# Loading the next input in four-row parts behind its scatters, in two standing buffers, with the weight stores one job later

## The chip, the cores and the metric

The kernel runs on one core of one Trainium2 chip. The metric is the device time of one execution in microseconds (us); a run's figure is the median over several executions. A core has TensorE (PE in the profile; its weight loads are PEld), VectorE (DVE), ScalarE (ACT), GpSimd (POOL) and SyncE (SP). SP issues most DMAs here and works its instructions off in order, so a DMA whose wait is not yet met holds all that stand behind it. POOL does the same with its own DMAs, the scatters and gathers.

## The reference

```python
X = np.fft.rfft(x, axis=1)                      # x: 8 inputs of 3072 rows x 256
Yr = Xr @ w_r - Xi @ w_i + b_r
Yi = Xr @ w_i + Xi @ w_r + b_i                  # then a soft threshold of 0.01 on both
y = np.fft.irfft(Y, n=3072, axis=1)             # 8 * 3072 = 24576 tokens
...
logits = xn @ en.T / tau                        # tokens routed to one of 8 experts
out[mask] = gate_w[mask, None] * (np.maximum(x[mask] @ w1[e], 0.0) @ w2[e])
...
h = x @ w_in                                    # dense layer over all tokens
return np.maximum(0.01 * h, h) @ w_out
```

## The kernel before

The program has three stages: the transform with the routing (up to about 910 us of the profile), the experts (to about 2173 us) and the dense layer (to the end). The change touches only the first, which takes the eight inputs b = 0 to 7 in turn.

An input has a **forward part**, `main_step(b, g)` for g = 0 to 25, and an **inverse part**, a loop over n2 = 0 to 36. `mix` (PE, L490) multiplies group g by the weights, ACT and DVE split the result into two halves (`split_evict`, L178 and L179), `s2` (L512) transforms it, DVE makes the threshold result `z` (L515 to L517), `s2i` (L528) starts back. In the inverse part PE transposes (`pv`, L540), finishes a row block n2 (`pyo`, L576), and DVE copies it into row n2 of the buffer `xt` of input b + 1 (L610), whose old content PE has read by then. The first transform of input b + 1 (`s1`, PE, L468) reads that buffer ahead of it: two row blocks each in the steps g = 24 and 25 and then one in each turn of the inverse loop, so that turn n2 reads row block n2 + 4. The first three steps of input b + 1 stand in the turns 31 to 33, so the forward loop proper begins with g = 3.

So a buffer `xt` goes through three uses: input b + 1 is loaded and read, the finished rows of input b are put in its place, and 32 indirect DMAs (`scatter`, POOL, L656) send them to their slots in DRAM while input b + 1 is worked on. From g = 3 to 24 a step issues one of them, two where g is a multiple of 3; the last two go out in the turns 5 and 6 of the inverse loop. A one-element copy on POOL (L655) holds each scatter until the `z` of the step before is there, which sets its pace. Input b + 2 can be loaded only where the rows have been scattered. In this version the pool `big` has two buffers of 16 row blocks; `load_x` takes a new one at q = 0 and 4, and such a buffer comes free as a whole. `refill` asks for the parts q = 0 to 3 (384 KB, four row blocks each) in the steps g = 21 to 24 and for 4 to 7 in the turns n2 = 4 to 7. Input 1 is loaded through the forward part of input 0, where no scatter goes out yet.

Beside it `split_job` prepares the experts' weights in 128 jobs, one a step up to g = 22 from input 0 on until none is left (in input 6). A job does three things in this order: SP loads a piece `wf` (128 KB, L451); then, for the piece of two jobs before, ACT makes the upper half of `hl` (L456), POOL the lower (L457); SP stores that `hl` (256 KB, L458). There are three buffers `wf` and four `hl`. On SP the store waits for POOL's half, on POOL that half stands behind the scatters of the step, and on ACT the upper half stands between the evictions that PE's results need.

Of the kernel before, what the change touches and what calls it, by code (L numbers as in the profile page):

```python
# [11 lines left out]
F32 = mybir.dt.float32  # L12
# [10 lines left out]
B, S, D = 8, 3072, 256  # L23
E = 8
T = B * S
N1, N2 = 96, 32
# [117 lines left out]
def build(ctx: ExitStack, tc: tile.TileContext, a: dict, out: bass.AP):  # L144
    nc = tc.nc
# [182 lines left out]
    def spectral(big, expert_start):  # L328
        with ExitStack() as st, ExitStack() as mst:
# [31 lines left out]

            xt = {}

            def load_x(b, q):
                if q % 4 == 0:
                    t = big.tile([128, 16, D], F32, tag="s", name="xt")
                    for j in range(4):
                        xt[b, q + j] = t[:N1, 4 * j:4 * j + 4, :]
                nc.sync.dma_start(
                    xt[b, q], x[b].rearrange("(p r) c -> p r c", r=N2)[:, 4 * q:4 * q + 4, :])  # L370

# [61 lines left out]
            jobs = []  # L433
            for e in range(E):
                for k in range(2):
                    for h in range(4):
                        o = k * 1024 + h * 256
# [4 lines left out]
                                 w2d[128 * e:128 * e + 128], f * 256))  # L442
            jobs.reverse()

            wait = []

            def split_job():
                if jobs:
                    src, dst, o = jobs.pop()
                    wf = m3.tile([128, 256], F32, tag="wf", name="wf")  # L450
                    nc.sync.dma_start(wf, src)  # L451
                    wait.append((wf, dst, o))
                if len(wait) == 3 or not jobs and wait:
                    wf, dst, o = wait.pop(0)
                    hl = m2.tile([128, 2, 256], F32R, tag="hl", name="hl", bufs=4)
                    nc.scalar.activation(hl[:, 0], wf, AF.Copy)  # L456
                    nc.gpsimd.tensor_tensor(hl[:, 1], wf, hl[:, 0], op=ALU.subtract)  # L457
                    nc.sync.dma_start(dst.rearrange("p (s n) -> p s n", s=2)[:, :, o:o + 256], hl.bitcast(F32))  # L458

            ps1 = {}  # L460

# [60 lines left out]
            def s2i(g):  # L522
                y = Y.pop(g)
                if g % 2 == 0:
                    pz[0] = psc.tile([128, 2, 2, 128], F32, tag="c", name="pz")
                p = pz[0]
                for db in range(2):
                    nc.tensor.matmul(p[:, db, g % 2, :], y[:, 128 * db:128 * db + 128], gi[:, g, :],  # L528
                                     start=True, stop=True)
                if g % 2 == 1:  # L530
                    nc.scalar.activation(
                        Z[:, :, :, 4 * g - 4:4 * g + 4],
                        p.rearrange("p b g (j n) -> p b n (g j)", n=N2), AF.Copy)
# [288 lines left out]


            LEAD = 2
            todo = []
            scat = []

            def main_step(b, g):
                last = b == B - 1
                if g == 3:  # L830

                    s2i(0)
                if g < NG:
                    mix(g)
                if 1 <= g <= NG:
                    s2(g - 1)
                if g >= NG and not last:
                    for _ in range(2):
                        s1(b + 1, lead[0])
                        lead[0] += 1  # L840
                if g >= 3:
                    s2i(g - 2)
                if b == 0 and g == 3:
                    todo.extend(prologue3())
                if g >= 3:
                    for _ in range(2):
                        if todo:
                            todo.pop(0)()
                if 2 <= g <= NG:
                    for _ in range(1 if g % 3 else 2):  # L850
                        scatter(Y[g - 1][0:1, 0:1])
                if 4 - (b > 0) <= g < 23:
                    split_job()
                if b == 0 and g % 3 == 1 and g // 3 < 8:
                    load_x(1, g // 3)
                if b and g in (21, 22, 23, 24):
                    refill(b + 1, g - 21)

            def scatter(step):
                if scat:  # L860
                    scat.pop(0)(step)
# [3 lines left out]
            def refill(b, q):  # L865


                if b < B:
                    load_x(b, q)
                elif q % 4 == 0:  # L870
                    w = q // 4
                    la[w][0] = big.tile([128, 4096], F32R, tag="s", name=f"W{w + 1}_0")
                    load_weights(0, w, la[w][0])
# [19 lines left out]
            for b in range(B):  # L893
# [4 lines left out]
                g0 = 0  # L898
                while lead[0] < LEAD and not last:
                    s1(b + 1, lead[0])  # L900
                    lead[0] += 1
                if last:
                    assert not jobs and not wait and not todo
                    mst.close()
                    yp = st.enter_context(tc.tile_pool(name="fy", bufs=1, reuse_waits="tile"))
                    y7.append(yp.tile([128, N2, D], F32, name="y7"))
                    ex = expert_start(la)
                    next(ex)
# [10 lines left out]
                for n2 in range(N2 + LAG + 2):  # L919
                    ready = len(squares)  # L920
                    copies()
                    if lead[0] < N2 and not last:
                        s1(b + 1, lead[0], later)
                        lead[0] += 1
                    if n2 < N2:
                        swap(n2, later)
                    if LAG <= n2 < N2 + LAG:
                        pend.append(s1i(b, n2 - LAG))
                    if ready:
                        squares.pop(0)()  # L930
                        if n2 < 10:
                            scatter(cur["ss"][0:1, n2 - LAG - 2:n2 - LAG - 1])
                    if n2 in (3, 9):
                        logits1(n2 // 9)
                    if n2 in (6, 12):
                        logits2(n2 // 12)
                    if n2 == 16:
                        logits = logits3()
                    if n2 == 17:
                        logits()  # L940
                        slots, sc, gates = routing(b)
                    if n2 > 17 and slots:
                        slots.pop(0)()
                    if n2 == 30:
                        assert not scat
                    if b and n2 in (4, 5, 6, 7):
                        refill(b + 1, n2)
                    if not last and n2 in MERGE:
                        copies()
                        main_step(b + 1, g0)  # L950
                        g0 += 1
                    if last and n2 >= 5 and n2 % 2 == 1:
                        copies()
                        next(ex)
# [195 lines left out]
    with tc.manual_schedule():  # L1150
        with ExitStack() as est:
# [7 lines left out]
            big = est.enter_context(tc.tile_pool(name="big", bufs=2, side="right"))  # L1159
# [38 lines left out]
```

## Time and profile before

| | |
|---|---|
| median of 3 runs | 4367.9 us (4366.33 to 4370.6) |
| the profiled execution, its own time | 4368.49 us |
| its span, first to last instruction | 4366.7 us |
| granted TensorE clock, mean over the span | 0.987 |
| PE busy / PEld / DVE / ACT / POOL | 98% / 87% / 55% / 43% / 14% |

The page cuts the span into 40 slices of 109 us each. PE is busy in nine tenths or more of nearly every slice, and the two lower digits are among the first eight slices, the stage that the change touches. The mean clock of 0.987 is not spread over the run either. A shared figure such as "98% busy" therefore says little about this stage: it is read in stretches of its own, one for each forward and each inverse part, by PE's busy time, the granted clock beside it, and the waits that ended PE's idle time. PE busy at half the clock counts as busy, so a stretch's length and its clock are read together.

### The profile page before, as it was taken

The page shows a single profiled execution, that of the slowest core. Times are in us where ns is not written, and L with a number is a line of the kernel's source. Part 1 is how long each engine was busy: PE and PEld are TensorE (multiplying, and loading weights), DVE is VectorE, ACT ScalarE, POOL GpSimd, SP SyncE. Part 2 cuts the span into 40 slices and gives each one's busy share as a digit, 9 for nine tenths or more (in the row PEclk, how much of TensorE's full clock was granted, in tenths as well). Part 3 has the DMA queues.
Part 4 walks back from the last instruction along what each step waited for, and adds up shares of the span by engine and source line. Part 5 has one row for each costly group of instructions (what it writes and reads, how often), then busy time and mean ns, then how long its engine had stood idle before and what let it go on. Part 6 is the DMA issues. An engine that isn't in the chain of part 4 may idle for free.

```text
span 4366.7 us, 72634 instructions
## 1 busy us (share of the span) xinstructions
PE 4271.0 (98%) x27214; PEld 3819.4 (87%) x27214; DVE 2391.4 (55%) x4977; ACT 1895.8 (43%) x4268; POOL 601.2 (14%) x893
## 2 busy tenths in 40 slices
PE   9989898999999999999999999999999999999999
PEld 8878787889999999999978888888888888888888
DVE  5777777763455555533355555555555555555554
ACT  4555555553333333333244444444444444444443
POOL 2443333424000000000010010100101000010100
PEclk9999999999999999999999999999999999999999
DMA  6343333242332225234100000000000000000000
GB/s 209 115 123 104 113 110 114 84 162 85 115 117 99 94 96 194 108 124 160 47 28 25 20 25 25 25 25 20 27 22 25 25 21 29 20 25 25 22 18 15
DMA packets 139074, 309.71 MB, mean 71 GB/s; under 512 B 21049, under 2 KB 72866, under 8 KB 134370
## 3 DMA queue, kind: packets, MB, share of 16 engines
q1 hardware_dynamic: 113250, 244.34, 16.6%
q0 software_dynamic: 25472, 60.73, 4.7%
q8 instruction: 215, 3.52, 0.4%
q14 instruction: 137, 1.12, 0.1%
HBM read 542.30 MB, written 115.02 MB: 151 GB/s over the span
## 4 chain that ended last, share of the span: by engine, by line
PE 88%; DVE 5%; DMA 2%; issue 2%; ACT 1%; POOL 1%; SPq 0%; another core or an unknown queue 0%; DVEq 0%; POOLq 0%; ACTq 0%
PE mpH L1035 24%; PE mpO L1060 16%; PE pO L272 14%; PE pH L256 14%; PE mpO L1061 8%; PE pu L490 3%; PE ps L468 2%; PE py L512 1%; PE pz L528 1%; DMA xt<-in_x_dram 1%; PE pyo L576 1%; DVE t L516 1%; DVE z L517 1%; DVE vl L543 1%; PE pT L240 1%
## 5 line engine op out<-in xcount | busy, mean ns | idle before, releaser
L1041 DVE TENSOR_TENSOR mg<-mpH,ms 128x512 f32<-128x512 f32 x768 | 531.4, 692 | 1046.5 <-ACT ms L1040 1041.1
L1060 PE MATMUL mpO<-W,mgh 128*128 128x512 f32 x3008 | 1095.9, 398 | 0.0
L1035 PE MATMUL mpH<-mxh,W 128*128 128x512 f32 x3072 | 1083.9, 394 | 4.8 <-DVE mg L1041 4.6
L1040 ACT ACTIVATE ms<-mpH 128x512 f32<-128x512 f32 x768 | 459.9, 599 | 1190.3 <-PE mpH L1035 977.6
L1061 PE MATMUL mpO<-W,mgl 128*128 128x256 f32 x3008 | 842.1, 280 | 0.0
L256 PE MATMUL pH<-xh,W 128*128 128x256 f32 x3296 | 728.9, 283 | 1.7 <-DMA W<-w1d 1.0
L1035 PEld LDWEIGHTS mpH<-mxh,W 128*128 128x128 f32 x3072 | 578.7, 188 | 144.2 <-DVE mg L1041 5.8
L1060 PEld LDWEIGHTS mpO<-W,mgh 128*128 128x128 f32 x3008 | 564.7, 188 | 132.4
L260 DVE SCALAR_TENSOR_TENSOR ehl<-pH,ehh 128x256 fp32r<-128x256 f32 x824 | 349.7, 425 | 600.7 <-ACT ehh L259 596.4
L259 ACT ACTIVATE ehh<-pH 128x256 fp32r<-128x256 f32 x824 | 316.3, 384 | 760.9 <-PE pH L256 743.6
L272 PE MATMUL pO<-W,ehh 128*128 128x256 f32 x3264 | 630.3, 285 | 0.4 <-issue 0.4
L1035 PE MATMUL mpH<-mxl,W 128*128 128x512 f32 x1536 | 606.7, 395 | 0.0
L1061 PEld LDWEIGHTS mpO<-W,mgl 128*128 128x128 f32 x3008 | 567.3, 189 | 24.9
L1008 POOL DMA_INDIRECT mxr<-ys,row x192 | 187.4, 976 | 2869.3 <-PE mpT L1020 1746.5
L256 PEld LDWEIGHTS pH<-xh,W 128*128 128x128 f32 x3296 | 573.7, 192 | 2.4 <-DMA W<-w1d 1.2
L1050 DVE TENSOR_TENSOR mgl<-mg,mgh 128x512 fp32r<-128x512 f32 x768 | 523.5, 682 | 0.0
L272 PEld LDWEIGHTS pO<-W,ehh 128*128 128x128 f32 x3264 | 508.2, 192 | 1.7 <-issue 1.7
L1049 ACT ACTIVATE mgh<-mg 128x512 fp32r<-128x512 f32 x768 | 479.0, 624 | 0.1
L256 PE MATMUL pH<-xl,W 128*128 128x256 f32 x1648 | 466.8, 283 | 0.0
L272 PE MATMUL pO<-W,ehl 128*128 128x256 f32 x1632 | 462.1, 283 | 0.9 <-issue 0.9
L1035 PEld LDWEIGHTS mpH<-mxl,W 128*128 128x128 f32 x1536 | 289.7, 189 | 33.1 <-DVE mxl L179 0.4
L256 PEld LDWEIGHTS pH<-xl,W 128*128 128x128 f32 x1648 | 316.5, 192 | 0.2 <-issue 0.2
(214 smaller groups left out, 5412.2 us busy)
## 6 DMA issues: line engine op xcount, KB each, us to landing
W<-w1d SPq DMA_DIRECT2D x101, 2048.0 KB
W<-w2d SPq DMA_DIRECT2D x101, 2048.0 KB
xg<-xs SPq DMA_DIRECT2D x103, 256.0 KB
ys<-eo SPq DMA_DIRECT2D x102, 256.0 KB
xt<-in_x_dram SPq DMA_DIRECT2D x64, 384.0 KB
out_dram<-mo SPq DMA_DIRECT2D x47, 512.0 KB
wf<-in_moe_w_dram SPq DMA_DIRECT2D x128, 128.0 KB
w1d<-hl SPq DMA_DIRECT2D x64, 256.0 KB
```

The costliest lines, as they stand in the source:

```text
L256: nc.tensor.matmul(p, l, r, start=(i == 0), stop=(i == 5))
L259: nc.scalar.activation(hh, p, AF.Relu)
L260: nc.vector.scalar_tensor_tensor(hl, p, 0.0, hh, op0=ALU.max, op1=ALU.subtract)
L272: nc.tensor.matmul(O[b][:, t, :], l, r, start=(f == 0 and i == 0 and t == 0), stop=(f == 7 and i == 2 and t == 1))
L1008: nc.gpsimd.indirect_dma_start(out=xr[i][:, t].bitcast(F32), out_offset=None, in_=ys, in_offset=IndirectOffsetOnAxis(ap=slot[:, 4 * i + t: ...
L1035: nc.tensor.matmul(p, l, r, start=(j == 0), stop=(j == 5))
L1040: nc.scalar.activation(s, p, AF.Copy, scale=0.01)
L1041: nc.vector.tensor_tensor(g, p, s, op=ALU.max)
L1049: nc.scalar.activation(gh, g, AF.Copy)
L1050: nc.vector.tensor_tensor(gl, g, gh, op=ALU.subtract)
L1060: nc.tensor.matmul(p, gh[:, c], wout[:, :, f], start=(f == 0), stop=False)
L1061: nc.tensor.matmul(p[:, 0], gl[:, c], wout[:, 0, f], start=False, stop=(f == 15))
```

## The change

The two buffers `xt` are now taken once and live through the stage, so that each part of four rows depends only on its own last users. The parts q = 0 to 6 of the next input but one are loaded in the steps g = 8, 11, 14, 17, 20, 22 and 25, two or three steps behind the scatter of their last row, and part 7 in turn 7 of the inverse loop. In the last input the first two expert weight buffers, which take the place of `xt`, are asked for at g = 17 and n2 = 7 instead of g = 21 and n2 = 4. A job's store is put into a list `done` and issued in the next job, behind that job's load of `wf`.

```diff
+            xbuf = [big.tile([128, 16, D], F32, tag="s", name="xt") for _ in range(2)]
+
             def load_x(b, q):
-                if q % 4 == 0:
-                    t = big.tile([128, 16, D], F32, tag="s", name="xt")
-                    for j in range(4):
-                        xt[b, q + j] = t[:N1, 4 * j:4 * j + 4, :]
+                xt[b, q] = xbuf[q // 4][:N1, 4 * (q % 4):4 * (q % 4) + 4, :]
                 nc.sync.dma_start(
                     xt[b, q], x[b].rearrange("(p r) c -> p r c", r=N2)[:, 4 * q:4 * q + 4, :])
...
-            wait = []
+            wait, done = [], []
...
                     wait.append((wf, dst, o))
+                if done:
+                    dst, o, hl = done.pop(0)
+                    nc.sync.dma_start(dst.rearrange("p (s n) -> p s n", s=2)[:, :, o:o + 256], hl.bitcast(F32))
                 if len(wait) == 3 or not jobs and wait:
                     wf, dst, o = wait.pop(0)
                     hl = m2.tile([128, 2, 256], F32R, tag="hl", name="hl", bufs=4)
                     nc.scalar.activation(hl[:, 0], wf, AF.Copy)
                     nc.gpsimd.tensor_tensor(hl[:, 1], wf, hl[:, 0], op=ALU.subtract)
-                    nc.sync.dma_start(dst.rearrange("p (s n) -> p s n", s=2)[:, :, o:o + 256], hl.bitcast(F32))
+                    done.append((dst, o, hl))
...
+            REFILL = (8, 11, 14, 17, 20, 22, 25)
...
-                if b and g in (21, 22, 23, 24):
-                    refill(b + 1, g - 21)
+                if b and g in REFILL:
+                    refill(b + 1, REFILL.index(g))
...
-                elif q % 4 == 0:
+                elif q % 4 == 3:
                     w = q // 4
...
-                    if b and n2 in (4, 5, 6, 7):
-                        refill(b + 1, n2)
+                    if b and n2 == 7:
+                        refill(b + 1, 7)
```

On SP, from g = 20 of input 1 to its inverse part, before (`xt` are the loads of input 2, `w1d<-hl` the stores; DMASW are the eight semaphores that the scatters use in turn, DMAHW those of SP's own DMAs):

```order
L451 DMA wf_2366<-in_moe_w1_dram 128x256 [waits DMAHW1_49]
L458 DMA w1d_57<-hl_2368 256x1x256 [waits DMAHW0_49,Pool_49]
L451 DMA wf_2402<-in_moe_w1_dram 128x256 [waits DMAHW3_49]
L458 DMA w1d_57<-hl_2404 256x1x256 [waits DMAHW2_49,Pool_49]
L369 DMA xt_2408<-in_x_dram 96x1024 [waits DMASW4_49,DMASW3_49,DMASW5_49,DMASW2_49,DMASW6_49,DMASW1_49,DMASW7_49,DMASW0_49,PE_49]
L451 DMA wf_2438<-in_moe_w1_dram 128x256 [waits DMAHW5_49,DMAHW4_49]
L458 DMA w1d_57<-hl_2440 256x1x256 [waits Pool_49]
L369 DMA xt_2408<-in_x_dram 96x1024 [waits DMAHW6_49]
L369 DMA xt_2408<-in_x_dram 96x1024 [waits DMAHW7_49]
L369 DMA xt_2408<-in_x_dram 96x1024 [waits DMAHW0_49]
L369 DMA xt_2582<-in_x_dram 96x1024 [waits DMASW4_49,DMASW5_49,DMASW3_49,DMASW6_49,DMASW2_49,DMASW7_49,DMASW1_49,DMAHW1_49,DMASW0_49,PE_49]
```

The same place after the change:

```order
L450 DMA wf_2367<-in_moe_w1_dram 128x256 [waits DMAHW3_49,DMAHW2_49,Pool_49]
L454 DMA w1d_57<-hl_2336 256x1x256
L368 DMA xt_136<-in_x_dram 96x1024 [waits DMASW2_49,DMASW3_49,DMASW1_49,DMAHW4_49,DMASW0_49,PE_49]
L450 DMA wf_2404<-in_moe_w1_dram 128x256 [waits DMAHW6_49,DMAHW5_49,Pool_49]
L454 DMA w1d_57<-hl_2370 256x1x256
L450 DMA wf_2438<-in_moe_w1_dram 128x256 [waits DMAHW7_49,DMAHW0_49,Pool_49]
L454 DMA w1d_57<-hl_2407 256x1x256
L368 DMA xt_136<-in_x_dram 96x1024 [waits DMASW6_49,DMASW7_49,DMASW5_49,DMAHW1_49,DMASW4_49,PE_49]
L368 DMA xt_136<-in_x_dram 96x1024 [waits DMASW2_49,DMASW3_49,DMASW1_49,DMAHW2_49,DMASW0_49,PE_49]
L368 DMA xt_136<-in_x_dram 96x1024 [waits DMASW6_49,DMASW7_49,DMASW5_49,DMAHW3_49,DMASW4_49,PE_49]
L665 DMA slotd_61<-mx_2841 96x32 [waits DMAHW4_49,DVE_49]
```

Here only the last four parts of input 2 are left, each waits for four scatters in place of eight, and the wait for POOL has gone from the store to the next load of `wf`.

On SP again, in the steps g = 6 to 9 of input 2, before:

```order
L451 DMA wf_3313<-in_moe_w2_dram 128x256 [waits DMAHW6_49,DMAHW5_49]
L458 DMA w2d_58<-hl_3315 256x1x256 [waits Pool_49]
L451 DMA wf_3347<-in_moe_w2_dram 128x256 [waits DMAHW7_49,DMAHW0_49]
L458 DMA w2d_58<-hl_3349 256x1x256 [waits Pool_49]
L451 DMA wf_3381<-in_moe_w2_dram 128x256 [waits DMAHW2_49,DMAHW1_49]
L458 DMA w2d_58<-hl_3383 256x1x256 [waits Pool_49]
L451 DMA wf_3417<-in_moe_w2_dram 128x256 [waits DMAHW5_49,DMAHW3_49]
```

After the change the same steps hold the first part of input 3:

```order
L450 DMA wf_3342<-in_moe_w2_dram 128x256 [waits DMAHW7_49,DMAHW6_49,Pool_49]
L454 DMA w2d_58<-hl_3311 256x1x256
L450 DMA wf_3376<-in_moe_w2_dram 128x256 [waits DMAHW1_49,DMAHW0_49,Pool_49]
L454 DMA w2d_58<-hl_3345 256x1x256
L368 DMA xt_135<-in_x_dram 96x1024 [waits DMASW2_49,DMASW3_49,DMASW1_49,DMAHW2_49,DMASW0_49,PE_49]
L450 DMA wf_3413<-in_moe_w2_dram 128x256 [waits DMAHW4_49,DMAHW3_49,Pool_49]
L454 DMA w2d_58<-hl_3379 256x1x256
```

A load of `xt` that waits for scatters now stands between two loads of `wf`; the stores stand behind the loads without a wait for POOL.

## Rows read from the trace of the kernel before

**Rows 1.** Waits of PE, inputs 1 to 6: waiter and releaser, total us, times, longest.

```profile
engine line waited for: us in total, times, longest us
PE ps L468 <- DMA xt<-in_x_dram: 30.9, 10, 5.4
PE pz L528 <- DVE z L517: 20.3, 41, 1.2
```

**Rows 2.** Windows: the inverse parts of the inputs 0 to 6, TensorE.

```profile
core 0: us, PE busy (x), PEclk, DMA share, GB/s
88.90:132.80 43.90, 41.57 (x358) 1.00 0.10 32
194.80:253.60 58.80, 49.89 (x358) 0.83 0.31 88
317.00:375.10 58.10, 50.33 (x357) 0.82 0.30 88
439.40:491.90 52.50, 44.52 (x358) 0.93 0.34 96
559.40:617.20 57.80, 50.55 (x357) 0.82 0.32 89
681.30:736.00 54.70, 45.73 (x357) 0.91 0.32 93
797.80:842.80 45.00, 41.80 (x358) 1.00 0.20 54
```

**Rows 3.** Windows: the forward parts of the inputs 1 to 6, same columns.

```profile
132.80:194.80 62.00, 59.65 (x365) 1.00 0.48 148
253.60:317.00 63.40, 59.96 (x366) 1.00 0.47 146
375.10:439.40 64.30, 59.95 (x366) 1.00 0.46 144
491.90:559.40 67.50, 62.42 (x364) 0.97 0.43 136
617.20:681.30 64.10, 59.97 (x365) 1.00 0.46 144
736.00:797.80 61.80, 59.44 (x367) 1.00 0.44 131
```

**Rows 4.** Timeline, input 1: SP's and PE's rows at the first load of input 2.

```profile
198.12 0.54 SPq L458 DMA_DIRECT2D w1d<-hl  x1
198.97 0.34 SPq L369 DMA_DIRECT2D xt<-in_x_dram  x1
...
203.64 0.74 PE L468 MATMUL ps<-f,xt 96*128 96x96 f32 x2 [4.94 <-DMA xt<-in_x_dram]
```

**Rows 5.** Windows of input 1 from that wait on, same columns.

```profile
198.70:203.60 4.90, 0.01 (x1) 0.67 0.87 243
203.60:217.40 13.80, 13.76 (x67) 0.50 0.35 104
```

**Rows 6.** Timeline: POOL's scatters of input 1 whose landing SP waits for.

```profile
150.46 0.92 POOL L656 DMA_INDIRECT xs<-xt,si  x1 [0.16 <-issue]
...
157.85 0.74 POOL L457 TENSOR_TENSOR hl<-wf,hl 128x256 fp32r<-128x256 f32 x1
...
222.44 0.92 POOL L656 DMA_INDIRECT xs<-xt,si  x1 [0.15 <-issue]
```

**Rows 7.** Timeline: the second four loads (SP), their first use, PE's rank product.

```profile
225.73 1.72 SPq L369 DMA_DIRECT2D xt<-in_x_dram  x4
...
229.61 0.66 PE L468 MATMUL ps<-f,xt 96*128 96x96 f32 x4 [1.91 <-DMA xt<-in_x_dram]
...
245.20 0.31 PE L650 MATMUL prk<-ob,tri 96*96 96x256 bf16 x1 [0.72 <-DVE ob L674]
```

**Rows 8.** Waits of ACT in the forward part of input 1.

```profile
ACT hl L456 <- DMA wf<-in_moe_w_dram: 9.9, 10, 2.2
```

**Rows 9.** Timeline, input 0: a load of input 1 ahead of a weight piece.

```profile
84.04 1.80 SPq L369 DMA_DIRECT2D xt<-in_x_dram  x1
85.95 0.36 SPq L451 DMA_DIRECT2D wf<-in_moe_w_dram  x1
...
89.81 0.42 ACT L456 ACTIVATE hl<-wf 128x256 fp32r<-128x256 f32 x1 [1.19 <-DMA wf<-in_moe_w_dram]
```

**Rows 10.** Timeline, input 1: a weight piece without such a load ahead.

```profile
182.10 0.60 SPq L451 DMA_DIRECT2D wf<-in_moe_w_dram  x1
...
185.25 0.42 ACT L456 ACTIVATE hl<-wf 128x256 fp32r<-128x256 f32 x1 [2.16 <-DMA wf<-in_moe_w_dram]
```

**Rows 11.** Timeline, input 4: a late scatter on POOL, then ACT, then PE.

```profile
517.76 0.93 POOL L656 DMA_INDIRECT xs<-xt,si  x1 [2.28 <-DVE t L516]
...
523.38 0.42 ACT L456 ACTIVATE hl<-wf 128x256 fp32r<-128x256 f32 x1 [3.35 <-DMA wf<-in_moe_w_dram]
...
527.14 0.71 PE L528 MATMUL pz<-gi,z 128*128 128x128 f32 x4 [1.22 <-DVE z L517]
```

**Rows 12.** Timeline, input 6: PE's wait at its second four loads.

```profile
820.27 0.66 PE L468 MATMUL ps<-f,xt 96*128 96x96 f32 x4 [0.88 <-ACT sq L618]
```

**Rows 13.** Windows behind the short waits in the inverse parts of inputs 2 and 4.

```profile
367.60:371.00 3.40, 3.40 (x19) 0.50 0.00 0
610.00:613.40 3.40, 3.40 (x19) 0.50 0.02 5
```

More of the change, by code (lines that the diff above doesn't have):

```diff
@@ L902, in spectral @@
                 if last:
-                    assert not jobs and not wait and not todo
+                    assert not jobs and not wait and not done and not todo
                     mst.close()
```

## The prediction

> **What bounds the kernel now.** PE sets the pace; the question is where it idles or runs slowly in the stage that the change touches. The waits of PE come first [rows 1]: over the inputs 1 to 6 it stood 30.9 us, in ten waits, for a load of `xt`, and 20.3 us, in 41 short ones, for `z`. The reader is to see that the first kind is few and long (two for each of the inputs 1 to 5), the second many and short.
>
> Next the same stretches by window. Seven inverse parts do the same work (357 or 358 PE instructions), yet take 43.9 us in input 0, 52.5 to 58.8 us in the inputs 1 to 5, and 45.0 us in input 6 [rows 2]. The two short ones run at a granted clock of 1.00, the five long ones at 0.82 to 0.93. Their excess over input 6 is 281.9 - 5 x 45.0 = 56.9 us, more than the 30.9 us waited. Split by PE's busy time: 241.0 - 5 x 41.8 = 32.0 us more of busy time and 24.9 us more of idle time. PE has the same matmuls, so the 32.0 us are matmuls run at the lower of the clock's two levels, 1.2 in place of 2.4 GHz. The window on input 1 shows when: in the 4.9 us wait the clock is 0.67 on average, behind it PE works 13.8 us at 0.50 [rows 5]. A wait for `xt` is thus paid twice.
>
> Why the load is late stands in the timeline [rows 4]. SP issues the first part at 198.97 us, just behind a store of `hl` at 198.12; PE wants it at 198.70 (203.64 less 4.94) and gets it 4.7 us after its issue. The store had waited for POOL, which runs behind the `z` of its step. Input 6, whose weight jobs run out halfway, issues its loads unhindered and shows no such wait at its first part; at its second four it has 0.88 us [rows 12]. Input 0, which loads input 1 all through its forward part, has neither, with jobs in nearly every step. These two are the templates for what the change makes of the five.
>
> **The change part by part.** *First four parts.* By the order on SP they now stand at g = 8, 11, 14 and 17, each behind a load of `wf` that waits for POOL's half of the step before. Is the wait for scatters then met? Row 3 of part 0 is scattered at 150.46 us; POOL's half of step g = 7 starts at 157.85 and takes 0.74 us [rows 6], so with two issues of 0.6 us (as in [rows 10]) SP arrives near 159.8, 9.3 us after that scatter. A scatter at 222.44 us let the next load go at 225.73, 3.3 us later [rows 6, 7]. The wait costs nothing, and the data, wanted at 198.7, are there some 35 us early. Gone: five waits of the kind of the 4.94 us.
>
> *Second four parts.* Before, all of them wait for the last scatter, and PE waits 1.91 us for the first [rows 7]. Now part 4 stands at g = 20, part 5 at 22, part 6 at 25, and only part 7 waits for row 31. That scatter stays where it is in its turn: at 222.44 us in input 1, so part 7 goes at about 225.7 and lands 3.9 us later (225.73 to 229.61), while its first use is turn 24, next to the rank product at 245.20 [rows 6, 7]: 15 us of cover. All five waits of this kind go, and input 6's 0.88 us as well, whose place is the same.
>
> *The clock.* With no wait of an `xt` left, the inverse parts should run as input 6's does. I take 56.9 us. To it comes 6 x 0.88 = 5.3 us, since the template has a wait that goes too (45.0 - 0.9 is 44.1, next to input 0's 43.9). Against it stand the short waits that stay: in two of the inverse parts 3.4 us at 0.50 follow other, shorter waits [rows 13], 1.7 us each; the same number of them should come back somewhere, 3.4 us. Together 58.8 us. Bounds: the waits alone, 30.9 us; and 5 x (56.38 - 43.9) + 1.1 = 63.5 us by input 0.
>
> The clock can also be priced by its own column: the missing share of each long part is 0.17 x 58.8 + 0.18 x 58.1 + 0.07 x 52.5 + 0.18 x 57.8 + 0.09 x 54.7 = 39.5 us [rows 2], with the waits 70.4 us, which would give 4298 us. I don't take it, since part of the low stretch lies in the wait itself, where there is nothing to slow (0.67 within it [rows 5]); the lengths say 56.9. The Trainium skill prices it in the first way: "TensorE: Matmul & The Clock Gate", section "Terms", gives the penalty as the throttled time times the share of the clock that is missing.
>
> *The weight jobs.* The load of `wf` now goes ahead of the store and waits for the same half on POOL as the store before it did, so it starts earlier by one issue, 0.6 us; the store goes 0.6 us later, and its buffer is wanted again only four jobs on. Gain: ACT waits 9.9 us for `wf` in input 1's forward part [rows 8], and these waits stand ahead of evictions that PE's `z` waits come from. The forward parts of the inputs 1 to 5 sum to 321.3 us, against 5 x 61.8 = 309.0 by input 6 [rows 3], so at most 12.3 us can be had. Loss: five loads of 384 KB (g = 8 to 20) now stand between the pieces of each of five forward parts; the others come behind the last job. In input 0 a piece behind such a load was used 3.86 us after its issue, in input 1 one without it 3.15 us after [rows 9, 10]: 0.7 us more, and 25 x 1.19 = 29.8 us if each cost what ACT waited there and all of it reached PE. The nearest row is input 1's own forward part: 9.9 us of such waits on ACT, and it is 0.2 us longer than input 6's [rows 3, 8]. So ACT's waits of about a microsecond are mostly absorbed. I take 0 for the jobs as a whole, between -12.3 and +29.8 us.
>
> Against the change speaks a rule of the Trainium skill, "DMA: Bandwidth & Descriptors", section "Queues, rings and completion order": on each DMA engine a ring's descriptors are consumed in order, so a small piece behind 384 KB starts late. The 0.7 us above agree with it. If all of that reached PE it would be 17.5 us, and by that rule the sum 4327 us.
>
> *The last input.* The two expert weight buffers are asked for in other steps, but their order on SP against its neighbours is the same and no job is left by then. Nothing moves: 0. The same holds for input 0, where only store and load change places.
>
> **The sum.** 4368.5 (the profiled execution's own time) - 58.8 + 0 = 4309.7 us. That execution lies 0.6 us above the median of the runs shown, so 4309 us.
>
> **The rivals.** *Only the waits go.* PE idles elsewhere, and the clock falls behind the `z` waits or the rank product's 0.70 us instead: 4368.5 - 30.9 = 4338. For it speak the two stretches of [rows 13]; against it the inputs 0 and 6, with the same short waits and a clock of 1.00.
>
> *Slower: the new loads hold SP.* A load of `xt` that has to wait for its scatters holds the next `wf`, ACT stands at that piece with the evictions behind it, and PE waits for `z`. Input 4 shows this chain once: POOL's scatter 2.28 us late, ACT 3.35 us at `wf`, PE 1.22 us at `pz` [rows 11], and that forward part is 67.5 us, 3.3 more than the mean (64.2) of the two on either side of it [rows 3]. At 3.3 us for each of 25 loads it is 82.5 us: 4368.5 - 58.8 + 82.5 = 4392. It decides against the change from 58.8 / 25 = 2.4 us of PE a load. Against it stands the lead of 9.3 us over a landing of 3.3; part 5, with two steps instead of three, has some 7.
>
> *In part the same:* the loads only delay the pieces by 0.7 to 1.19 us [rows 9, 10], and between two thirds and all of it reaches PE: 25 x 0.5 to 25 x 1.19, 4322 to 4339.
>
> *The buffers are still freed as a whole.* Then part 0 would wait at g = 8 for scatters that stand later, and nothing would be gained: about 4368. The order excludes it nearly: each part waits for four scatter semaphores where the old load waited for eight.
>
> *More comes back:* the clock's whole missing share, 4298, or the forward parts go to input 6's 61.8 us too, 4309.7 - 12.3 = 4297.
>
> **How the numbers follow.** The forecast, 4300 to 4322, has 0.70; only the waits 0.07; the loads eat a part 0.08; more comes back 0.08; nothing happens 0.03; slower 0.04. The range 4298 to 4334 holds the forecast and most of its neighbours. What a measurement of this kernel can tell from no change is about 0.2%, 8.7 us: faster 0.93, same 0.03, slower 0.04.
>
> **What would show it.** Right: no wait of PE for `xt` in the inputs 1 to 5, inverse parts of 44 to 46 us at a clock near 1.00, first parts issued 30 us and more ahead of their use. ACT's wait for `wf` in a forward part should stay near 9.9 us and the forward parts near 62 to 64. Wrong: low clock in the inverse parts without such waits (the clock's cause was another), forward parts of 66 us and more with long ACT waits at the piece behind each part (the queue), or SP standing at the loads of `xt` for scatters in the forward part.

## The result

The changed kernel takes 4302.7 us (median; 4300.0 to 4310.8) against 4369.3 us (4366.3 to 4375.1) for the kernel before on the same chip: a ratio of 0.9846 [0.9832, 0.9860], 67 us less where 59 were forecast (4309, range 4298 to 4334). Its profiled execution took 4302.98 us, with a span of 4301.2 us, 65.5 less than before.

The first answer is that of the waits of PE over the inputs 1 to 6 (waiter and releaser, total us, times, longest), to be laid beside [rows 1]. No wait for `xt` is left, while the many short waits for `z` are what they were, 20.6 us against 20.3:

```profile
PE pz L530 <- DVE z L519: 20.6, 43, 1.1
PE prk L652 <- DVE ob L676: 4.3, 6, 0.7
```

Next the windows of the inverse parts of the inputs 0 to 6 (us, PE busy and instructions, granted clock, DMA share, GB/s), against [rows 2]. All but the first now take the same 43.9 us at a clock of 1.00:

```profile
89.70:134.90 45.20, 43.15 (x358) 0.96 0.06 18
197.60:241.50 43.90, 41.55 (x358) 1.00 0.25 74
305.40:349.30 43.90, 41.56 (x357) 1.00 0.25 74
413.10:457.00 43.90, 41.56 (x357) 1.00 0.25 74
522.10:566.00 43.90, 41.55 (x357) 1.00 0.25 76
629.60:673.50 43.90, 41.54 (x357) 1.00 0.25 76
735.50:779.40 43.90, 41.56 (x358) 1.00 0.17 46
```

And the forward parts of the inputs 1 to 6, against [rows 3]. They moved more data per second, and took as long as before:

```profile
134.90:197.60 62.70, 59.68 (x365) 1.00 0.58 177
241.50:305.40 63.90, 59.94 (x365) 1.00 0.57 173
349.30:413.10 63.80, 60.02 (x366) 1.00 0.57 174
457.00:522.10 65.10, 60.45 (x363) 1.00 0.56 169
566.00:629.60 63.60, 60.02 (x366) 1.00 0.56 172
673.50:735.50 62.00, 59.37 (x367) 1.00 0.47 141
```

So the account of the span is: the inverse parts of the inputs 1 to 5 fall from 281.9 to 219.5 us (-62.4), input 6's by 1.1; the forward parts of the inputs 1 to 6 fall from 383.1 to 381.1 (-2.0); input 0 takes 2.3 more (its inverse part is 45.2 in place of 43.9, its forward part 59.9 in place of 58.9); the rest of the program takes 2.3 less. The 62.4 us split as the prediction split them: PE's busy time in the five parts falls from 241.0 to 207.8 us (-33.2, matmuls no longer run at the lower level) and its idle time from 40.9 to 11.7 (-29.2).

The timeline of SP (start us, us, queue, line, operation) shows the first part of input 2 behind a load of `wf` and the store of the job before, and PE's row its first use 39 us later. Of SP's waits from the start of this forward part to the end of the inverse part, two are shown: it stands for POOL at the loads of `wf`, as it stood at the stores before, and at the loads of `xt` only twice for scatters (`xs`), both in the inverse part, where nothing wanted is behind. In the forward parts of the inputs 2 to 5 it doesn't wait for a scatter either; in input 6's it does, 8.4 us, with no weight job left behind it:

```profile
161.30 0.33 SPq L450 DMA_DIRECT2D wf<-in_moe_w_dram  x1
161.67 0.55 SPq L454 DMA_DIRECT2D w1d<-hl  x1
162.75 0.12 SPq L368 DMA_DIRECT2D xt<-in_x_dram  x1
```

```profile
201.77 0.61 PE L470 MATMUL ps<-f,xt 96*128 96x96 f32 x4
```

```profile
SPq L450 <- POOL dummy L657: 37.0, 12, 13.1
SPq L368 <- DMA xs<-xt,si: 9.3, 2, 8.8
```

### The profile page after: what moved, and what is told of

Its sections match the earlier page's. It is cut to its first block, busy times and chain, and to the rows that moved or that the text cites. A ratio compares the mean times of both kernels' runs of the same rounds, so it can differ in the third digit from the quotient of the medians.

```text
span 4301.2 us, 72806 instructions
## 1 busy us (share of the span) xinstructions
PE 4234.7 (98%) x27214; PEld 3789.6 (88%) x27214; DVE 2387.1 (55%) x4977; ACT 1894.3 (44%) x4268; POOL 597.0 (14%) x893
## 4 chain that ended last, share of the span: by engine, by line
PE 91%; DVE 4%; issue 2%; ACT 1%; DMA 1%; POOL 0%; SPq 0%; another core or an unknown queue 0%; ACTq 0%; DVEq 0%; POOLq 0%
PE mpH L1039 25%; PE mpO L1064 16%; PE pO L272 14%; PE pH L256 14%; PE mpO L1065 8%; PE pu L492 4%; PE ps L470 2%; PE py L514 2%; PE pyo L578 2%; PE pz L530 1%; PE pv L542 1%; DVE t L518 1%; PE pT L240 1%; PE mpT L1024 1%; DVE z L519 1%
## 5 line engine op out<-in xcount | busy, mean ns | idle before, releaser
L256 PEld LDWEIGHTS pH<-xl,W 128*128 128x128 f32 x1648 | 316.3, 192 | 1.2 <-issue 1.2
```

The costliest lines, as they stand in the source:

```text
L256: nc.tensor.matmul(p, l, r, start=(i == 0), stop=(i == 5))
```

## The experiments

Three questions were put. Which half of the change carries the gain, and does it need the early steps? Is it the wait that buys the low clock? And since the forward parts hardly moved although SP's order changed in all of them: what does PE wait for there? The kernels of one group ran on one chip, beside runs of the kernel before (medians 4361.5, 4366.9 and 4357.9 us for the three groups), so the ratios are compared, not the times. "Inverse" is the sum of the inverse parts of the inputs 1 to 5, "forward" that of the forward parts of the inputs 1 to 6, in the profiled execution. Input 4's forward part takes from 61.6 to 67.9 us in all kernels but `e8_lower_half_on_dve` and doesn't follow the edits, so the last column gives the sum of the other five, which is steadier.

| kernel | median us | ratio to before [95%] | inverse | forward | forward without input 4 |
|---|---|---|---|---|---|
| before | 4369.3 | 1 | 281.9 | 383.1 | 315.6 |
| changed | 4302.7 | 0.9846 [0.9832, 0.9860] | 219.5 | 381.1 | 316.0 |
| e1_loads_only | 4307.8 | 0.9875 [0.9859, 0.9892] | 222.0 | 383.5 | 317.3 |
| e2_stores_only | 4342.4 | 0.9957 [0.9940, 0.9973] | 261.6 | 377.5 | 315.9 |
| e3_fill | 4347.0 | 0.9965 [0.9951, 0.9979] | 256.2 | 383.2 | 316.8 |
| e4_parts_late | 4332.6 | 0.9933 [0.9917, 0.9950] | 248.5 | 378.2 | 316.5 |
| a0_after (the changed kernel again) | 4307.6 | 0.9871 [0.9851, 0.9891] | 219.4 | 380.6 | 315.5 |
| e5_wf_four | 4304.4 | 0.9857 [0.9839, 0.9876] | 222.5 | 378.2 | 316.3 |
| e6_t_two_inputs | 4306.5 | 0.9864 [0.9845, 0.9884] | 220.7 | 381.5 | 316.7 |
| e7_same_step | 4313.3 | 0.9879 [0.9860, 0.9897] | 222.6 | 389.0 | 321.1 |
| e8_lower_half_on_dve | 4266.0 | 0.9793 [0.9777, 0.9809] | 219.4 | 355.2 | 296.0 |
| e9_job_before_scatter | 4280.6 | 0.9827 [0.9811, 0.9843] | 219.4 | 369.6 | 306.2 |

**The two halves apart.** The changed kernel with each store back in its own job, and the kernel before with the stores one job later:

```diff
-                if done:
-                    dst, o, hl = done.pop(0)
-                    nc.sync.dma_start(... hl.bitcast(F32))
...
-                    done.append((dst, o, hl))
+                    nc.sync.dma_start(... hl.bitcast(F32))
```

> The changed kernel with the store of hl back in its own job, behind POOL's half: the loads in parts alone. If the loads carry the gain: no wait of PE for xt, inverse parts of 43.9 us at a clock of 1.00, and 4302 to 4308 us; ACT's wait for wf in a forward part back from 4.4 to about 10 us, without effect on PE. If the later store carries part of it: waits for xt return or the forward parts grow by 2 us each, 4313 us or more.

> The kernel before with the store of hl one job later and nothing else. The first load of the next input then stands behind a load of wf that waits for POOL's half of the step before, so it should be issued near 195 us in input 1 instead of 198.97: the five first waits fall from 4.0 to 5.4 us to about 1 us each, the five second ones (1.1 to 1.9 us) stay. If the low clock is bought by the waits, most of its cost goes as well: some 19 us of waits and 10 to 20 us of clock, 4330 to 4340 us. If only the loads' place matters: 4365 us, no change.

The loads alone give what the change gives: 0.9875 against 0.9871 and 0.9846 for the two takes of the changed kernel, no wait of PE for `xt`, inverse parts of 43.9 to 45.2 us. The store's move on top of them brings nothing that can be told. On the kernel before it brings about 19 us, a little less than the 4330 to 4340 us expected: PE still waits 22.0 us for `xt` (30.9 before), and the five inverse parts are 20.3 us shorter. There, by SP's order, the loads of `xt` no longer stand behind a store that waits for POOL; where they are issued dozens of microseconds early, that lead has no use. The halves don't add up (54 and 19 us alone, 59 to 67 together), as both take from the same waits.

**Is it the steps?** The changed kernel, standing buffers and all, with the loads asked for where they were before:

```diff
-            REFILL = (8, 11, 14, 17, 20, 22, 25)
+            REFILL = (21, 22, 23, 24)
...
-                    if b and n2 == 7:
-                        refill(b + 1, 7)
+                    if b and n2 in (4, 5, 6, 7):
+                        refill(b + 1, n2)
```

> The changed kernel with the loads back in their old steps (g = 21 to 24, n2 = 4 to 7): standing buffers and the later store stay. Part 0 is issued behind the load of wf of g = 21, near 195 us in input 1, so a first wait of about 1 us is left in each of the inputs 1 to 5; part 4 no longer waits for row 31, so the second waits go. With some of the clock: 4308 to 4322 us. If the early steps are needed for the clock: first waits with low clock behind them, 4325 us or more.

It landed in the second range, 4325 us or more: 0.9933, some 29 us gained, about half of the whole. The waits of PE for `xt` in the inputs 1 to 6 of this kernel, and the two of them that fall in input 1, on PE's timeline:

```profile
PE ps L470 <- DMA xt<-in_x_dram: 15.1, 10, 3.4
```

```profile
201.12 1.13 PE L470 MATMUL ps<-f,xt 96*128 96x96 f32 x8 [1.26 <-DMA xt<-in_x_dram]
...
205.79 0.69 PE L470 MATMUL ps<-f,xt 96*128 96x96 f32 x4 [1.73 <-DMA xt<-in_x_dram]
```

Both are for the first two parts, and so are the other eight; the waits at the second four loads [rows 7] are gone, though these are asked for in the same turns as before. So the change has two gains of like size: buffers that come free in parts with stores that don't hold SP, and the early steps. And the waits that are left are, in sum, paid twice here too. Beside the changed kernel the inverse parts are 29.0 us longer: 15.1 us of it waited (over the inputs 1 to 6), and PE's busy time 15.5 us longer (223.3 against 207.8). Not every wait is: in input 3, behind waits of 0.5 and 2.0 us, the clock stayed at 1.00 (46.5 us), and so it did with the stores alone in input 1, behind waits of 2.7 and 1.1 us:

```profile
193.90:242.60 48.70, 42.06 (x357) 1.00 0.35 98
```

**Does the wait buy the low clock?** The kernel before, with matmuls that write to a tile nobody reads, put where PE waits for the first and the second four loads. They add work to the kernel; nothing of it is used:

```diff
+            def fill(n):
+                pf = psc.tile([128, 512], F32, tag="c", name="pf")
+                for _ in range(n):
+                    nc.tensor.matmul(pf, wh[:, 0, 0:128], wh[:, 0], start=True, stop=True)
...
+                if g == NG and 0 < b < B - 2:
+                    fill(16)
...
+                    if n2 == 12 and 0 < b < B - 2:
+                        fill(4)
```

> The kernel before with matmuls whose result nobody reads: 16 ahead of the first s1 of the next input at g = 24 and 4 ahead of turn 12 of the inverse part, in the inputs 1 to 5, where PE stood idle for xt. The loads are as late as before. If the wait buys the low clock: the clock of the inverse parts goes from 0.82 to 0.93 to nearly 1.00, the time PE stands at xt (idle and filled) stays near 31 us, and some 25 us are gained: about 4344 us. If the low clock has another cause: clock as before, and 4369 us or a few more.

The timelines of SP and of PE in input 1: the load is as late as in [rows 4], 4.1 us into the inverse part (202.56 us) against 4.2 there, and the sixteen matmuls stand where PE stood idle:

```profile
202.56 0.34 SPq L369 DMA_DIRECT2D xt<-in_x_dram  x1
```

```profile
202.24 3.80 PE L827 MATMUL pf<-wh 128*128 128x512 f32 x16
206.41 1.13 PE L468 MATMUL ps<-f,xt 96*128 96x96 f32 x8 [0.37 <-DMA xt<-in_x_dram]
```

The windows of its inverse parts of the inputs 1 to 5:

```profile
198.50:248.50 50.00, 46.66 (x377) 1.00 0.37 102
312.50:363.10 50.60, 46.64 (x377) 1.00 0.36 100
426.50:476.90 50.40, 46.62 (x378) 1.00 0.36 102
543.30:593.80 50.50, 46.61 (x377) 1.00 0.35 100
658.00:712.70 54.70, 49.60 (x377) 0.94 0.33 93
```

PE does twenty matmuls more in each part and is 25.7 us faster over the five, at a clock of 1.00 in four of them, with the data no earlier. That settles the cause for these stretches: the low clock followed from PE standing idle in the wait, not from the transfer beside it or from where the stretch lies. By the medians of its own group the gain is about 15 us (0.9965), less than the 21.6 between the two profiled spans, which come from different groups, so its size is less sure than its sign. That 6 to 7 us are left in each of the four against 43.9 is the wait itself, now filled (4.9 us of matmuls in input 1) or still idle (9.8 us in ten waits over the five). In input 5 the low stretch doesn't stand behind a wait for `xt`: it begins 2.5 us behind the rank product, for which PE had stood 0.7 us, and is of the kind of [rows 13]:

```profile
704.80:711.60 6.80, 6.80 (x35) 0.50 0.00 0
```

**The price of a load that stands in the queue.** The rival on the other side was that a load of `xt` that waits for its scatters holds the weight pieces. To see it at work the loads were put closer to their scatters, three steps earlier (two for the last two):

```diff
-            REFILL = (8, 11, 14, 17, 20, 22, 25)
+            REFILL = (5, 8, 11, 14, 17, 20, 23)
```

> The changed kernel with each part loaded in the very step of its last scatter (g = 5, 8, 11, 14, 17, 20, 23), so SP has to stand there until that scatter has landed, 3 to 5 us, with the next load of wf behind it. By the prediction's slower rival ACT waits 2 to 3 us for that piece five times a forward part and PE loses up to 3.3 us each time: 4320 to 4385 us. If ACT's waits hardly reach PE: 4300 to 4312 us, with ACT's wait for wf at 10 us or more in a forward part.

ACT's waits over the inputs 1 to 6 of this kernel, and of the changed one:

```profile
ACT hl L458 <- DMA wf<-in_moe_w_dram: 74.0, 52, 4.9
```

```profile
ACT hl L458 <- DMA wf<-in_moe_w_dram: 30.9, 41, 2.0
```

The mechanism exists: in input 1's forward part SP stands 16.9 us for scatters at the loads, where it stood for none, and over the six inputs ACT waits 43 us more for the pieces. But PE's time shows little of it. The forward parts are 7.9 us longer (5.1 without input 4), the median 5.7 us above the changed kernel's beside it and just above the lower of the two ranges expected, and the intervals of the two ratios overlap. Over 25 loads that is 0.2 to 0.3 us each, where the rival had 3.3; it is a net figure, as the counts further down show.

**What PE waits for in the forward part.** The changed kernel with a fourth buffer for the pieces, so that a piece is used three jobs behind its load:

```diff
-                    wf = m3.tile([128, 256], F32, tag="wf", name="wf")
+                    wf = m3.tile([128, 256], F32, tag="wf", name="wf", bufs=4)
...
-                if len(wait) == 3 or not jobs and wait:
+                if len(wait) == 4 or not jobs and wait:
```

> The changed kernel again, beside the next three on one chip: 4300 to 4306 us, no wait of PE for xt, inverse parts of 43.9 us.

> The changed kernel with four buffers wf instead of three and a piece used three jobs behind its load instead of two. ACT's wait for wf (4.4 to 5.5 us in a forward part) goes. If PE's waits for z come from it, as the prediction took it: they fall from 20.6 us (43 times) to less than 8, and the time goes to about 4293 us. If they come from DVE's tensor_scalar t, which takes up to 1.51 us instead of 0.29 while POOL is at work: they stay near 20 us, 4300 to 4306 us.

The second take of the changed kernel gave the ratio 0.9871 [0.9851, 0.9891], with 43.9 us in every inverse part. With the fourth buffer ACT's wait for `wf` is gone, all 30.9 us of it, and the forward parts without input 4 are as long as before (316.3 us against 316.0 and 315.5); the median is 3 us lower than that of the second take, within the intervals. PE's waits over the inputs 1 to 6:

```profile
PE pz L530 <- DVE z L519: 14.3, 35, 0.6
PE pz L530 <- issue: 4.3, 6, 0.8
```

So these waits are not made by ACT's wait for the pieces: most of them stay without it (14.3 and 4.3 us, against 20.6). The timeline of DVE in the changed kernel gave another lead, and POOL's beside it (same columns):

```profile
158.88 0.41 DVE L517 TENSOR_TENSOR z<-py,bt 128x256 f32<-128x256 f32 x1
159.33 0.29 DVE L518 TENSOR_SCALAR t<-z 128x256 f32<-128x256 f32 x1
...
161.44 0.41 DVE L517 TENSOR_TENSOR z<-py,bt 128x256 f32<-128x256 f32 x1
161.89 1.51 DVE L518 TENSOR_SCALAR t<-z 128x256 f32<-128x256 f32 x1
```

```profile
161.54 0.92 POOL L658 DMA_INDIRECT xs<-xt,si  x1 [0.16 <-issue]
162.48 0.76 POOL L459 TENSOR_TENSOR hl<-wf,hl 128x256 fp32r<-128x256 f32 x1
```

The operation that makes `t` takes 0.29 us at 159.33 and 1.51 us at 161.89, and the second ends just behind POOL's subtraction for `hl` (162.48 + 0.76). Grouped by line over input 1's forward part (minimum, median and maximum in ns), the sum that reads PSUM is never long, the two that read SBUF alone are, now and then:

```profile
L517 DVE TENSOR_TENSOR z<-py,bt x22: 406/415/416, 139.4 to 197.5; 128x256 f32<-128x256 f32 x22
L518 DVE TENSOR_SCALAR t<-z x21: 293/295/1507, 139.9 to 195.1; 128x256 f32<-128x256 f32 x21
L519 DVE TENSOR_TENSOR z<-z,t x21: 424/426/1567, 140.2 to 196.6; 128x256 f32<-128x256 f32 x21
```

Over the inputs 1 to 6, 54 operations of these two lines took over 0.6 us, and every one of them ran beside a subtraction on POOL; 58 did before the change. They are also what `z` is late by: in the forward parts, counted row by row, 44 of PE's 45 waits ahead of `pz` (21.2 of 21.5 us) end at a `z` of which one of the two operations had taken over 0.6 us, and 41 of 42 (20.4 of 20.7 us) before the change. Three kernels go after it. The first makes `t` in another form of instruction, with two operands in SBUF (the constant's tile and its filling are left out below); the second lets POOL do its half ahead of the step's scatter; the third has DVE do it, and POOL not at all:

```diff
...
-                nc.vector.tensor_scalar(t, z, LAM, -LAM, op0=ALU.min, op1=ALU.max)
+                nc.vector.scalar_tensor_tensor(t, z, -LAM, lamt[:, 0:1].to_broadcast([128, D]), op0=ALU.max,
+                                               op1=ALU.min)
...
```

```diff
+                if 4 - (b > 0) <= g < 23:
+                    split_job()
                 if 2 <= g <= NG:
...
-                if 4 - (b > 0) <= g < 23:
-                    split_job()
```

```diff
-                    nc.gpsimd.tensor_tensor(hl[:, 1], wf, hl[:, 0], op=ALU.subtract)
+                    nc.vector.tensor_tensor(hl[:, 1], wf, hl[:, 0], op=ALU.subtract)
```

> The changed kernel with t made by a scalar_tensor_tensor against a broadcast constant instead of a tensor_scalar with two constants; the same values. If the tensor_scalar is held by POOL: t takes about 0.43 us each time, none above 0.6, PE's waits for z fall from 20.6 us to less than 8, and the time goes to about 4292 us. If the waits come from ACT's wait for wf: t costs 0.14 us more each, hidden, and the time stays at 4300 to 4306 us.

> The changed kernel with the step's weight job recorded ahead of its scatters, so POOL's subtraction no longer stands behind a scatter that waits for z. The next load of wf then goes out 2 to 3 us earlier and ACT's wait for it in a forward part falls from 4.4 us to below 2. If PE's waits for z came from ACT: they fall below 10 us. If they come from POOL's subtraction beside DVE: the long t and z stay as many (some 50), the waits stay near 20 us and the time at 4300 to 4308 us.

> The changed kernel with the lower half of hl made on DVE instead of POOL, where it took 0.74 us. In the changed kernel all 54 of DVE's t and z operations that took over 0.6 us instead of 0.29 to 0.43 ran beside POOL's subtraction. If that subtraction holds them: none above 0.6 us is left, and DVE has 20 x 0.43 = 8.6 us more work in a forward part of 62 us. PE's waits for z (20 us) fall below 8 and the time to 4290 to 4297 us if these holds are what z is late by; if DVE's queue takes up what the holds gave, the time stays at 4300 to 4308 us.

The other form changes nothing: 49 long operations in place of 54, forward parts of 381.5 us. With the job ahead of the scatter 26 are left, and the forward parts are 11.5 us shorter (9.8 without input 4); neither of its expectations came true, PE's waits for `z` lying between the two:

```profile
PE pz L530 <- DVE z L519: 13.6, 23, 1.4
```

With the subtraction on DVE none is left. The line of `t` in input 1's forward part of that kernel, PE's waits for `z` over the inputs 1 to 6, and the windows of the forward parts 1, 2 and 6:

```profile
L518 DVE TENSOR_SCALAR t<-z x21: 293/294/486, 138.3 to 190.3; 128x256 f32<-128x256 f32 x21
```

```profile
PE pz L530 <- DVE z L519: 2.5, 11, 0.3
```

```profile
133.30:192.00 58.70, 58.43 (x365) 1.00 0.63 198
235.90:295.10 59.20, 58.70 (x364) 1.00 0.63 198
648.50:707.90 59.40, 58.90 (x366) 1.00 0.48 148
```

The forward parts fall from 381.1 to 355.2 us (by 20.0 without input 4, which now takes 59.2 like the others), and the waits for `z` from 20.6 to 2.5. DVE has more to do and PE waits less for it. At 0.9793 [0.9777, 0.9809] this version beats both kernels: some 26 us more than the change brought, by the forward parts. By the medians it would be 37 us; but its group ran on a chip where the kernel before was faster too, and where the stretch behind input 6's inverse part, which its edit doesn't touch, takes 3511 us against 3522 in the changed kernel's profile. The ratios (0.9793 against 0.9846 and 0.9871) put it at 23 to 34 us. Both ranges expected lie above its 4266 us; that is 4279 us if its ratio is taken of 4369, still below them.

The counts bear on the kernel with the closer loads too. In it 31 operations took over 0.6 us, and yet PE's waits for `z` stayed:

```profile
PE pz L530 <- DVE z L519: 18.5, 41, 1.2
```

Of its 42 waits ahead of `pz` in the forward parts (18.9 us), 22 (11.7 us) end at a held `z`, the other 20 (7.2 us) at one that wasn't. So the late pieces do reach PE, and the fewer holds hide a part of it. Without that relief a load would cost some 0.7 us, by an estimate from these counts (7.9 us, and the 9.5 us by which the waits at a held `z` fell, over 25 loads); that is still far from 3.3.

The Trainium skill has the hold as a rule. "SBUF — State Buffer", section "Who interferes with whom", says that a VectorE instruction in a two-port mode, or one with two inputs in SBUF, contends with a GpSimd instruction that reads SBUF, that one of the two then blocks fully, and that an instruction with at most one SBUF input outside these modes doesn't. The rows agree as to who is held: line 519, with two inputs in SBUF, is, and line 517, with one input in PSUM, is not (416 ns at most). Line 518 is held too; that it ran in a two-port mode, as the rule would have it, no run shows. By that rule the kernel with the other form could not tell anything apart, since both forms are of the kind that can be held.

The length of a hold isn't explained so simply. The operations are up to 1.2 us longer (1.51 in place of 0.29), the subtraction takes 0.74; and 31 of the 54 began before it, by up to 0.6 us, as at 161.89 against 162.48, beside the scatter that POOL did first. By the profile POOL's times are rough, and beside scatters alone, in the kernel with the subtraction on DVE, no operation of the two lines took over 0.49 us. Whether a scatter adds to a hold stays open. Of the 26 us that went with the subtraction, 18.9 are idle time of PE (21.6 to 2.7 us), close to the 21.2 us of waits at a held `z`; the other 7.0 are PE's busy time (359.5 to 352.5 us), and what they come from, POOL's shorter queue included, was not tried.

## Why the prediction was right, and where it was not

**The inverse parts, -56.9 and -5.3.** Right in mechanism and size. The template was input 6 less its one wait, 44.1 us; the parts came to 43.9. The two terms gave 62.2 us for the inverse parts of the inputs 1 to 6, and 63.5 went. The row of input 6's wait names ACT as the one that ended it [rows 12]; it was read as a wait for the load, and it went with the late loads. That the low stretches were paid for by the wait was an inference from where they stood [rows 4, 5]; the filled wait showed it by itself. Pricing by lengths in place of the clock's missing share was right too: the share gave 39.5 us for the slow matmuls, PE's busy time fell by 33.2. The Trainium skill's formula ("TensorE: Matmul & The Clock Gate", section "Terms"), the throttled time by the missing share, is the pricing by share; it is 6 us above the 33.2 here. Part of the low stretch lies in the waits, which fits that: 0.67 within the first [rows 5].

**Two short low stretches come back, +3.4.** Mis-sized. In the profiled execution one came back, in input 0's inverse part (45.2 us, clock 0.96), at a cost of 1.3 us; in the second take of the changed kernel none did, all seven parts being 43.8 or 43.9. They come and go between executions; the copy with the old stores had two, the one with loads closer to their scatters four in its inverse parts. So the two takes give 1.3 us and nothing in place of 3.4. Of the 6.7 us by which the sum was above the profiled execution, this is 2.1; the inverse parts give 1.3, the forward parts 2.0 and the rest of the program 2.3, less 1.0 for input 0's forward part.

**Early enough, and no wait for scatters.** Right. Part 0 was issued at 162.75 us, where 159.8 was expected; the whole stretch begins 2.1 us later than before (134.9 against 132.8), so 0.9 us were missed. It led its use by 39 us, and SP waited for no scatter in the forward parts of the inputs 1 to 5.

**The weight jobs, 0 between -12.3 and +29.8.** The value was right (-2.0), the reason given for its bounds was wrong in one step. ACT's waits for `wf` were said to stand ahead of the evictions that PE's waits for `z` come from. Over four kernels ACT waits 0, 31, 62 and 74 us (the fourth buffer, the change, the old stores, the closer loads), and the forward parts without input 4 take 316.3, 316.0, 317.3 and 321.1 us: by these sums nothing of the first 31 us reaches PE, and of the next 43 a net 5 us. The waits for `z` came mostly from DVE being held beside POOL, a cause that stood in the trace of before (58 long operations) and that the prediction didn't look for, since the waits of PE end at DVE and DVE was read as waiting in its turn. The bound of -12.3 us, a like stretch of another input, was for that reason no bound of what can be had there: 26 us can. That the value came out right was thus partly luck: the change happens to leave POOL's subtractions beside DVE's operations (54 long ones against 58).

**ACT's wait would stay near 9.9 us.** Wrong, without cost: in input 1's forward part it fell to 4.4 us and 3.6 us for POOL came in its place. ACT's waits at `hl` there, against [rows 8]:

```profile
ACT hl L458 <- DMA wf<-in_moe_w_dram: 4.4, 7, 1.5
ACT hl L458 <- POOL dummy L657: 3.6, 3, 1.6
```

The store's move does that. ACT's wait for `wf` over the inputs 1 to 6, in the kernel before, with the loads alone and with the stores alone (30.9 us with both):

```profile
ACT hl L456 <- DMA wf<-in_moe_w_dram: 59.0, 53, 3.4
ACT hl L455 <- DMA wf<-in_moe_w_dram: 62.4, 53, 3.1
ACT hl L459 <- DMA wf<-in_moe_w_dram: 18.5, 28, 1.5
```

So the 25 loads cost ACT 3.4 us with the old stores, 0.14 us each, and 12.4 us with the moved ones, 0.5 us each; the 0.7 us read from one pair of rows [rows 9, 10] was somewhat high. The ring rule of the Trainium skill ("DMA: Bandwidth & Descriptors", "Queues, rings and completion order") would have given 4327 us with that price; the runs show the effect on ACT and, at the steps chosen here, none on PE that can be told.

**The rivals.** *Only the waits go* (4338): out, the clock is 1.00 in all six parts. *Slower* (4392): its chain can be made to run, and costs 0.3 us a load net, some 0.7 without the fewer holds, in place of 3.3; the late scatter of input 4 [rows 11] was a poor row to price it by, since that forward part is long with and without the early loads (67.5 us before, 65.1 after, 67.9 with the closer loads) and short in three other kernels, again with and without them (61.6 to 61.9: the stores alone, the late parts, the fourth buffer). *In part the same* (4322 to 4339): out, the forward parts got no longer. *Freed as a whole* (4368): out by the issue times. *More comes back* (4297 to 4298): the result lies between it and the forecast.

## What to carry to other kernels

Price a wait of TensorE by the length of the stretch against a like stretch without it: here the waits cost, in sum, about as much again at the lower clock (30.9 us waited, 33.2 us of busy time gone with them), though not each of them, and filling the wait with useless matmuls won back a part with the data no earlier. A buffer that is refilled in the parts in which it comes free, with transfers placed some steps behind their releaser, cost PE nearly nothing here, even where it went ahead of other pieces in the queue. And where an engine ends many short waits, look at the longest duration of its operations beside the median before looking for what it waits for: here an operation that was now and then five times as long was being held while another engine worked beside it.

## What the runs showed of the hardware

Not expected: operations of DVE on operands in SBUF grew from 0.29 or 0.43 us to as much as 1.57 us beside POOL's elementwise subtraction, which itself takes 0.74 us, in both forms of instruction tried; with the subtraction away the forward parts fell by 26 us of 381, some 19 of it PE's waits for the held results. Without the subtraction, beside scatters alone, 0.49 us was the longest of line 518 in input 1's forward part. And the granted clock stayed at 1.00 in stretches in which PE stood idle in short waits often, up to 1.1 us each, while the one low stretch of the changed kernel's inverse parts (3.4 us at 0.50, from 127.4 us) begins 2 us behind input 0's rank product, for which PE had stood 0.7 us. The other rank products, with the same wait, have none; which of the short waits lowers the clock was not settled.
